# Fewer and larger transfers in a fused attention and state-space kernel

## The chip, the cores and the metric

The kernel runs on one core of one Trainium2 chip. The metric is the device time of one execution in microseconds (us). The engines of the core are PE (matrix multiplication), ACT (activation functions), DVE (elementwise work), POOL, and SP, whose instruction queue issues nearly all DMA transfers here. DMA transfers run beside the engines.

## The reference

Two branches of 2048 rows by 512 columns are mixed by a gate.

```python
g = sigmoid((x * gate_w).sum(-1, keepdims=True))
# branch A: attention, 32 heads of 16, no mask
q, k, v = split(x @ wqkv)
a = softmax(q @ k.T * 16 ** -0.5) @ v  @ wo
# branch B: state-space convolution of u = x over the sequence, per channel d
P = exp(dt * A * l)                      # powers l = 0..2047 of 128 states
K[d, l] = real(sum_n C[d,n] * P[d,n,l] * dt * B[d,n])
b = causal_conv(x, K) + x * Dskip        # written with an FFT
out = g * a + (1 - g) * b
```

Attention has 32 x 2048 x 2048 scores, and each needs an exponential. Branch B is computed in chunks of 64 rows: a short convolution inside the chunk ("taps"), a state per chunk that is carried on by a scan, and the state's part of the output by powers of the state matrix.

## The kernel before, in words

**Attention.** A block `b` (0 to 31) is 512 queries (`qc`) and four of a group of eight heads (`pi`, by parity `w`): 64 score tiles of 128 keys by 512 queries. The main loop (from line 1716) runs over 683 groups of three score tiles. `qk` (line 890) writes a group to PSUM with K = 32 matmuls: two heads of 16 rows share 32 rows, and `Qm` holds the queries of one of them, with zeros in the rows of the other. `ex` (line 905) is one ACT instruction, the exponential of the group's tiles. `pv` multiplies by V. Some tiles are taken from ACT: a "set" of four tiles is turned into bits of the exponential by DVE (`bits`, line 941, four instructions at line 945, and two at line 956). Which groups give a tile to DVE is settled by `decide` while the program is written, by the time that the planned DVE has left.

**Branch B.** `table` (line 1211) makes the powers of two blocks of 32 channels in `PT` and stores them in memory, `ptd`. `kstage` (line 1265) makes the taps of a block of 32 channels and stores them in `kpd`. `sstage` makes the chunk states, `scan` carries them on, in two halves of 8 blocks, on DVE. `ystage` (line 1384) is the output: 32 units of 16 channels. A unit needs its powers `Py` (from `ptd`), its taps `Tt` (from `kpd`, read as overlapping rows so that each partition is shifted by one), and `XY`, a turned copy of x for four blocks, from `xrd`. It makes 32 small matmuls with powers and 16 with taps into the PSUM bank `MB`, one DVE instruction (line 1420) into `Yst`, and stores to `ytd`, from which `yread` transposes into `Yl`. `turned` (line 1453) builds in memory, `xcd`, copies of x with zeros at their side, for the states.

**Order of the work.** Nothing is scheduled on the chip: the program of each engine is a fixed list, and an instruction waits on semaphores for what it reads. The lists are written by a planner (class `Sched`, line 282). Threads such as `ystage`, `yloads`, `qms`, `xyloads`, `turned` yield an engine and a cost; `fill` picks the piece that can start first by planned times, then by priority (line 1704: a smaller number goes first), and `AFTER` names a mark that must have been written already. The costs are the `c=` and `lat=` arguments, and a DMA is planned to be ready `DMARG` = 2.4 us later than that. So a change of a transfer's cost or number also changes where other work is put. After the writing, `place` finds addresses in SBUF by the life of each buffer. Where `want` finds too little matmul work, the planner puts in matmuls on zeros (`zero`, from `wm`).

The SP queue is one list in order. An SP instruction whose semaphore isn't there holds all that stand behind it. Loads of the Y stage have priority 4 and `XY` loads too; `ystage`'s own pieces, its stores among them, have 2; Q rows have 0.

Lines that the change touches: `yload` and `yloads` (1361 to 1382), the stores at 1426, `mk_qm` at 737, the store of Q at 1605, the taps' store at 1282, the zero stores at 1457 and the XR stores at 1467.

Of the kernel before, what the change touches and what calls it, by code (L numbers as in the profile page):

```python
# [13 lines left out]
P = 128  # L14
S = 2048
D = 512
# [24 lines left out]
YR = 4  # L41
# [373 lines left out]
def declare(nc, es):  # L415
# [89 lines left out]

    sb("Py", YR * 2 * 16 * T)
    sb("Tt", YR * 8 * 64)
# [6 lines left out]
    for n, free in (("ptd", NBLK * P * 2 * CB * T), ("kpd", NBLK * P * 8 * P), ("xrd", S * D), ("xcd", 2 * S * D), ("ytd", D * S), ("qd", D * S), ("od", D * S)):  # L514
        B[n] = Buf(n, "dr", free, BF16)
        B[n].t = nc.dram_tensor("gm_" + n, [free // P, P], BF16)
# [95 lines left out]
def record(nc, p, B, ins):  # L612
# [118 lines left out]
    def mk_qm(b, j):  # L731
# [4 lines left out]
        else:  # L736
            dma("SP", lambda e: e.dma_start(Qm(512 * w, [[1, 512]], 32 * j + 16 * w, 16),
                                            B["qd"].dram(((4 * qc + pi) * P + 32 * j + 16 * w) * 512, [[512, 16], [1, 512]])),
                [(B["qd"], (pi, qc))], [(Qm, (w, j), b)], c=.62, lat=2.8)
# [525 lines left out]
    def kstage(blk):  # L1265
# [16 lines left out]
        dma("SP", lambda e: e.dma_start(kpd.dram(blk * P * 8 * P, [[8 * P, P], [1, 8 * P]]), Kst(1024 * (blk % 2), [[1, 8 * P]])),  # L1282
# [76 lines left out]
    YN = 2 * 16 * T  # L1359

    def yload(u):
        blk, hf = divmod(u, 2)
        r = u % YR
        yield ("SP", .5)
        dma("SP", lambda e: e.dma_start(Py(r * YN, [[16 * T, 2], [1, 16 * T]]),
                                        ptd.dram(blk * P * PTN + hf * 16 * T, [[PTN, P], [CB * T, 2], [1, 16 * T]])),
            [(ptd, blk)], [(Py, r, u)], c=.62, lat=3.8)
        for par in range(2):
            for a in range(2):
                yield ("SP", .4)  # L1370
                dma("SP", lambda e, par=par, a=a: e.dma_start(  # L1371
                    Tt(r * 512 + 256 * a, [[64, 4], [1, 64]], 64 * par, 64),
                    kpd.dram(blk * P * 8 * P + (2 * hf + a) * 40 * 8 * P + par * 9 * P, [[1, 64], [18 * P, 4], [1, 64]])),
                    [(kpd, blk)], [(Tt, (r, par, a), u)], c=.64, lat=2.8)
        sch.mark(f"yl{u}")

    def yloads():
        yield ("AFTER", "S15")
        for u in range(2 * NBLK):
            if u >= YR:  # L1380
                yield ("AFTER", f"yu{u - YR}")
            yield from yload(u)

    def ystage():
        def unit(u):
# [3 lines left out]
            r, r2 = u % YR, u % 4  # L1389
            yield ("AFTER", f"scan{h}")  # L1390
            yield ("AFTER", "gt")
            yield ("AFTER", f"yl{u}")
# [7 lines left out]
            for q in range(4):  # L1400
                yield ("PE", .15)
                for ri in range(2):
                    for j in range(4):
# [3 lines left out]
                           lambda ri=ri, i=i: Py(r * YN + ri * 16 * T + i * T, [[1, T]]),  # L1407
                           [(sg, b_, (h, 'G')) for b_ in range(32)] + [(sg, "z"), (Py, r, u)], ky, False, False,
                           pos=(0, 32 * j), c=.075 if j == 0 else 0, a=16, cfg="C")
            for q in range(4):  # L1410
                yield ("PE", .09)
                for j in range(4):
# [3 lines left out]
                       lambda k=k, par=par: Tt(r * 512 + 64 * k, [[1, 64]], 64 * par, 64),  # L1416
                       [(B[f"XY{qr}"], par), (Tt, (r, par, k // 4), u)], ky, False, True, pos=(64 * par, 32 * j), c=.085 if j == 0 else 0, a=8,
# [6 lines left out]
            for par in range(2):  # L1424
                yield ("SP", .45)
                dma("SP", lambda e, par=par: e.dma_start(ytd.dram((256 * par + 8 * u) * S, [[T, 64], [2 * S, 4], [1, T]]), Yst(r2 * 256, [[64, 4], [1, 64]], 64 * par, 64)),
                    [(Yst, r2, u)], [(ytd, (u, par))], c=.6, lat=3.2)
# [390 lines left out]
```

## Time and profile before

| | |
|---|---|
| time, median of 3 runs | 838.77 us (838.6 to 840.81) |
| profiled execution | span 837.7 us; its own time isn't shown apart from the span |
| ACT busy | 819.1 us, 98% of the span |
| DVE busy | 783.3 us, 94% |
| PE busy | 698.3 us, 83% |
| PE granted clock, mean | 0.991 |
| DMA | 94.90 MB, 248465 packets, mean 113 GB/s |

The span runs from the first to the last instruction. "Busy" is the union of an engine's instructions; PE's share counts matmuls that overlap and that are there only to keep the engine at work. In the rows of groups stand the line, the engine, the operation, output and inputs by the program's names, shape and count; then busy time and mean duration of one in nanoseconds (two instructions can overlap, so busy divided by count is the pace); then the idle time of the engine just before, and what ended it. In the order of time, a row starts with its start and its length in us, and merges neighbours (x4); a bracket at its end is idle time before it. "SPq" is the issuing of a DMA by SP, not the transfer. Rows of stretches give, for each engine, busy us and number of instructions.

### The profile page before, as it was taken

The page shows a single profiled execution, that of the slowest core. Times are in us where ns is not written, and L with a number is a line of the kernel's source. Part 1 is how long each engine was busy: PE and PEld are TensorE (multiplying, and loading weights), DVE is VectorE, ACT ScalarE, POOL GpSimd, SP SyncE. Part 2 cuts the span into 40 slices and gives each one's busy share as a digit, 9 for nine tenths or more (in the row PEclk, how much of TensorE's full clock was granted, in tenths as well). Part 3 has the DMA queues.
Part 4 walks back from the last instruction along what each step waited for, and adds up shares of the span by engine and source line. Part 5 has one row for each costly group of instructions (what it writes and reads, how often), then busy time and mean ns, then how long its engine had stood idle before and what let it go on. Part 6 is the DMA issues. An engine that isn't in the chain of part 4 may idle for free.

```text
span 837.7 us, 21043 instructions
## 1 busy us (share of the span) xinstructions
PE 698.3 (83%) x8982; PEld 253.4 (30%) x8982; DVE 783.3 (94%) x1344; ACT 819.1 (98%) x695; POOL 11.0 (1%) x13
## 2 busy tenths in 40 slices
PE   7877777787679888887788887788897779999996
PEld 3232332122122332332232332244342224333332
DVE  5799999999889998999999999999899999999996
ACT  7999999999999999999999999999999999999996
POOL 4000000000000000000000000000000000000000
PEclk9999999999999999999999999999999999999999
DMA  9650044792361976873392846045564414544113
GB/s 207 142 83 10 23 77 92 202 228 57 128 177 46 223 123 179 119 205 67 139 144 40 143 67 143 1 108 136 140 148 109 115 54 110 135 99 132 34 45 101
DMA packets 248465, 94.90 MB, mean 113 GB/s; under 512 B 223156, under 2 KB 235316, under 8 KB 246324
## 3 DMA queue, kind: packets, MB, share of 16 engines
q1 hardware_dynamic: 246500, 92.51, 49.6%
q8 instruction: 70, 1.15, 0.5%
q10 hardware_dynamic: 1872, 1.05, 0.5%
q14 instruction: 23, 0.19, 0.1%
HBM read 33.08 MB, written 35.01 MB: 81 GB/s over the span
## 4 chain that ended last, share of the span: by engine, by line
ACT 83%; DVE 7%; PE 5%; DMA 3%; SPq 0%; issue 0%; ACTq 0%; DVEq 0%
ACT ET L909 83%; PE SC L628 2%; PE OA L628 2%; DVE tt L1006 2%; DMA gm_ptd<-PT 2%; DVE PT L1006 1%; DMA Wk<-in_A_wqkv_dram 1%; DVE DZ L945 1%; PE MB L628 1%; DMA XY<-gm_xrd 1%; DVE DZ L956 0%; DVE s L1336 0%; DVE OT L980 0%; DVE s L1338 0%; SPq L1371 0%
## 5 line engine op out<-in xcount | busy, mean ns | idle before, releaser
L909 ACT ACTIVATE ET<-SC 128x1536 bf16<-128x1536 f32 (+1 forms) x683 | 810.8, 1537 | 5.9 <-PE SC L628 3.6
L628 PE MATMUL SC<-Qm,KT 32*128 32x512 bf16 x2048 | 276.1, 387 | 122.4 <-ACT ET L909 107.7
L628 PE MATMUL OA<-wm 128*32 128x512 bf16 (+3 forms) x1374 | 204.1, 365 | 1.2 <-DVE wm L681 1.2
L945 DVE TENSOR_SCALAR DZ<-SC 128x512 uint16<-128x512 f32 x256 | 170.1, 684 | 10.3 <-PE SC L628 9.4
L628 PE MATMUL OA<-ET,VE 128*32 128x512 bf16 x1792 | 179.7, 394 | 0.0
L628 PEld LDWEIGHTS SC<-Qm,KT 32*128 32x128 bf16 x2048 | 70.9, 91 | 339.8 <-ACT ET L909 303.1
L628 PEld LDWEIGHTS OA<-ET,VE 128*32 128x32 bf16 x1792 | 45.7, 93 | 102.0 <-issue 97.6
L628 PEld LDWEIGHTS OA<-wm 128*32 128x32 bf16 (+2 forms) x1374 | 54.6, 95 | 25.9 <-issue 17.7
L956 DVE TENSOR_SCALAR DZ<-DZ 128x2048 uint16<-128x2048 uint16 x64 | 43.8, 684 | 3.0 <-PE OA L628 2.7
L1309 DVE TENSOR_SCALAR SG<-MB 128x512 bf16<-128x512 f32 x64 | 43.7, 684 | 3.0 <-DMA gm_ptd<-PT 1.7
L956 DVE TENSOR_SCALAR DU<-DZ 128x2048 uint16<-128x2048 uint16 x64 | 43.1, 684 | 0.1
L628 PE MATMUL MB<-X,Qt 128*128 128x64 bf16 x512 | 42.1, 244 | 1.2 <-DVE SG L1309 1.2
L1344 DVE TENSOR_TENSOR G<-s,s 128x512 f32<-128x512 f32 x60 | 41.3, 688 | 1.1
L1338 DVE TENSOR_TENSOR s<-G,MU 128x512 f32<-128x512 f32 x60 | 41.1, 684 | 0.0
L1341 DVE TENSOR_TENSOR s<-s,SG 128x512 f32<-128x512 f32 x60 | 41.0, 683 | 0.0
L1336 DVE TENSOR_TENSOR s<-G,MU 128x512 f32<-128x512 f32 x60 | 40.9, 682 | 0.0
L628 PEld LDWEIGHTS MB<-X,Qt 128*128 128x128 bf16 x512 | 28.8, 116 | 20.0 <-issue 20.0
L1006 DVE TENSOR_TENSOR ft<-FP,L 128x1024 f32<-128x1024 f32 (+1 forms) x32 | 34.4, 1086 | 0.2
L1006 DVE TENSOR_TENSOR PT<-tt,tt 128x1024 bf16<-128x1024 bf16 x48 | 32.9, 685 | 0.5
L628 PEld LDWEIGHTS MB<-Py,SG 128*32 128x32 bf16 x1024 | 27.8, 168 | 6.8 <-issue 4.1
L628 PE MATMUL MB<-Py,SG 128*32 128x64 bf16 x1024 | 28.6, 231 | 0.0
L1347 DVE CAST SG<-G 128x512 bf16<-128x512 f32 x60 | 25.3, 422 | 1.1
(167 smaller groups left out, 613.9 us busy)
## 6 DMA issues: line engine op xcount, KB each, us to landing
gm_ptd<-PT SPq DMA_DIRECT2D x16, 1024.0 KB, 5.9
Py<-gm_ptd SPq DMA_DIRECT2D x32, 512.0 KB, 4.3
gm_kpd<-Kst SPq DMA_DIRECT2D x16, 256.0 KB, 3.1
Tt<-gm_kpd SPq DMA_DIRECT2D x128, 32.0 KB, 3.2
gm_xrd<-in_A_x_dram SPq DMA_DIRECT2D x1, 2048.0 KB, 13.7
gm_xcd<-wm SPq DMA_DIRECT2D x4, 512.0 KB, 10.4
gm_xcd<-XR SPq DMA_DIRECT2D x32, 64.0 KB, 1.9
Wo<-in_A_wo_dram SPq DMA_DIRECT2D x4, 512.0 KB, 3.8
```

Of the source, the lines that this page charges most:

```text
L628: op("PE", lambda t: t.matmul(out(), lhsT(), rhs(), start=start, stop=stop, skip_group_check=True, **kw), R, W, c=c, lat=.15, a=a, cfg=cfg)
L909: op("ACT", lambda a: a.activation(ET(512 * e, [[1, 512 * n]]), sc(0, [[1, 512 * n]]), AF.Exp, scale=DH ** -0.5), [(sc, i, g) for i in ran ...
L945: op("DVE", lambda v: v.tensor_scalar(z.u16(512 * k, [[1, 512 * n]]), sc(512 * na, [[1, 512 * n]]), XS, XB, ALU.mult, ALU.add), [(sc, na + ...
L956: op("DVE", lambda v: v.tensor_scalar(t.u16(0, [[1, 2048]]), z.u16(0, [[1, 2048]]), float(STEP[k][0]), None, ALU.add), R, W, c=.07 + 2048 ...
L1006: op(eng, lambda v: v.tensor_tensor(o(), a(), b_(), f), R, W, c=c)
L1309: op("DVE", lambda v, kh=kh, part=part: v.tensor_scalar(sg(2 * SGH + SGH * part + CB * k8 + 16 * kh, [[2 * SGH, 32], [1, 16]]), MB(0, [[16 ...
L1336: op(e, lambda v: v.tensor_tensor(s2(0, W), G(0, W), MU(d0, [[0, 2], [1, 256]]), ALU.mult), key("G", "MU"), [(s2, 0)], c=F5)
L1338: op(e, lambda v: v.tensor_tensor(s3(0, W), G(256, [[-256, 2], [1, 256]]), MU(D + d0, [[D, 2], [1, 256]]), ALU.mult), key("G", "MU") + [(M ...
L1341: op(e, lambda v, so=so: v.tensor_tensor(s2(0, W), s2(0, W), sg(so, [[SGH, 2], [1, 256]]), ALU.add), [(s2, 0)] + ks, [(s2, 0)], c=F5)
L1344: op(e, lambda v: v.tensor_tensor(G(0, [[1, 512]]), s2(0, [[1, 512]]), s3(0, [[1, 512]]), ALU.add), [(s2, 0), (s3, 0)], [(G, 0)], c=F5)
L1347: op(e, lambda v, so=so: v.tensor_copy(sg(so, [[SGH, 2], [1, 256]]), G(0, W)), key("G"), ks if c < NCH - 2 else [(sg, k, (h, 'G')) for k i ...
```

## The change

1. **Taps and powers by blocks.** `yload` (per unit: one `Py` load of 512 KB, four `Tt` loads of 32 KB) is replaced by loads per block of two units: one `Py` load of 1 MB and two `Tt` loads, each 64 partitions by 16 channels. The ring holds two blocks where it held four units, in the same space; a block is loaded after the last unit of the block before last. For that, `kpd` is laid out with the 32 channels as outer rows.
2. **Outputs by two units.** `ytd` is stored once per block and half (two DMAs), after the second unit, where there were two DMAs per unit.
3. **Masked Q in one load.** `qd` is doubled: 16 rows of zeros stand behind the 16 rows of each head. One DMA loads all 128 partitions of `Qm`, zeros and data, where four DMAs loaded 16 rows each. A new thread, `gaps`, writes zeros once at the start (2 MB, over the gaps); a Q load reads both keys.
4. **Zeros of the turned x.** Four zero stores of 64-element rows, which left out the places of the data, become two stores of 512-element rows that cover everything (2 MB each); they are written after `blk2`, and the stores of `XR` now wait for them.

The diff, cut to its core:

```diff
-YR = 4
...
-    sb("Py", YR * 2 * 16 * T)
-    sb("Tt", YR * 8 * 64)
+    sb("Py", 2 * 2 * CB * T)
+    sb("Tt", 2 * 16 * 64)
...
-    def mk_qm(b, j):
+    def mk_qm(b):
...
-            dma("SP", lambda e: e.dma_start(Qm(512 * w, [[1, 512]], 32 * j + 16 * w, 16),
-                                            B["qd"].dram(((4 * qc + pi) * P + 32 * j + 16 * w) * 512, [[512, 16], [1, 512]])),
-                [(B["qd"], (pi, qc))], [(Qm, (w, j), b)], c=.62, lat=2.8)
+            dma("SP", lambda e: e.dma_start(Qm(512 * w, [[1, 512]]),
+                                            B["qd"].dram(((4 * qc + pi) * 256 + 16 * w) * 512, [[64 * 512, 4], [512, 32], [1, 512]])),
+                [(B["qd"], (pi, qc)), (B["qd"], "z")], [(Qm, (w, j), b) for j in range(4)], c=.62, lat=2.8)
...
-        dma("SP", lambda e: e.dma_start(kpd.dram(blk * P * 8 * P, [[8 * P, P], [1, 8 * P]]), Kst(1024 * (blk % 2), [[1, 8 * P]])),
+        dma("SP", lambda e: e.dma_start(kpd.dram(blk * P * 8 * P, [[8 * P, 4], [32 * P, 32], [1, 8 * P]]), Kst(1024 * (blk % 2), [[1, 8 * P]])),
...
     def yloads():
         yield ("AFTER", "S15")
-        for u in range(2 * NBLK):
-            if u >= YR:
-                yield ("AFTER", f"yu{u - YR}")
-            yield from yload(u)
+        for blk in range(NBLK):
+            r = blk % 2
+            if blk >= 2:
+                yield ("AFTER", f"yu{2 * blk - 3}")
+            yield ("SP", .5)
+            dma("SP", lambda e, blk=blk, r=r: e.dma_start(Py(r * PTN, [[1, PTN]]), ptd.dram(blk * P * PTN, [[PTN, P], [1, PTN]])),
+                [(ptd, blk)], [(Py, r, blk)], c=.66, lat=4.8)
+            for par in range(2):
+                yield ("SP", .4)
+                dma("SP", lambda e, blk=blk, r=r, par=par: e.dma_start(
+                    Tt(r * 1024, [[64, 16], [1, 64]], 64 * par, 64),
+                    kpd.dram(blk * P * 8 * P + par * 33 * P, [[1, 64], [66 * P, 16], [1, 64]])),
+                    [(kpd, blk)], [(Tt, (r, par), blk)], c=.66, lat=3.4)
+            sch.mark(f"yl{blk}")
...
-            for par in range(2):
-                yield ("SP", .45)
-                dma("SP", lambda e, par=par: e.dma_start(ytd.dram((256 * par + 8 * u) * S, [[T, 64], [2 * S, 4], [1, T]]), Yst(r2 * 256, [[64, 4], [1, 64]], 64 * par, 64)),
-                    [(Yst, r2, u)], [(ytd, (u, par))], c=.6, lat=3.2)
             if hf == 1:
+                for par in range(2):
+                    yield ("SP", .45)
+                    dma("SP", lambda e, par=par: e.dma_start(ytd.dram((256 * par + 16 * blk) * S, [[T, 64], [2 * S, 8], [1, T]]),
+                                                             Yst((r2 - 1) * 256, [[64, 8], [1, 64]], 64 * par, 64)),
+                        [(Yst, r2 - 1, u - 1), (Yst, r2, u)], [(ytd, (blk, par))], c=.66, lat=3.4)
...
+    def gaps():
+        yield ("SP", .7)
+        dma("SP", lambda e: e.dma_start(B["qd"].dram(16 * 512, [[32 * 512, P], [512, 16], [1, 512]]), wm(0, [[0, 16], [1, 512]])),
+            [(wm, 0)], [(B["qd"], "z")], c=1.4, lat=8.)
+
     def turned():
         XR, xcd = B["XR"], B["xcd"]
-        for z in range(4):
-            yield ("SP", .6)
-            dma("SP", lambda e, z=z: e.dma_start(xcd.dram(z // 2 * P * 8192 + z % 2 * 4096 + 64 * (1 - z % 2), [[8192, P], [P, 32], [1, 64]]), wm(0, [[0, 32], [1, 64]])),
-                [(wm, 0)], [(xcd, ("z", z))], c=.6, lat=6.)
+        yield ("AFTER", "blk2")
+        for z in range(2):
+            yield ("SP", 1.4)
+            dma("SP", lambda e, z=z: e.dma_start(xcd.dram(z * P * 8192, [[8192, P], [512, 16], [1, 512]]), wm(0, [[0, 16], [1, 512]])),
+                [(wm, 0)], [(xcd, ("z", z))], c=1.4, lat=10.)
         yield ("AFTER", XAT)
...
-                    [(XR, (c % 2, i), c) for i in range(2)], [(xcd, (c, cc))], c=.5, lat=3.)
+                    [(XR, (c % 2, i), c) for i in range(2)] + [(xcd, ("z", cc % 2))], [(xcd, (c, cc))], c=.5, lat=3.)
...
-                dma("SP", lambda e, i=i, c=c: e.dma_start(B["qd"].dram((4 * c + i) * P * 512, [[512, P], [1, 512]]), B["Qs"](512 * i, [[1, 512]])),
+                dma("SP", lambda e, i=i, c=c: e.dma_start(B["qd"].dram((4 * c + i) * 256 * 512, [[32 * 512, 8], [512, 16], [1, 512]]), B["Qs"](512 * i, [[1, 512]])),
...
-                for j in range(4):
-                    yield ("SP", .62, 0)
-                    mk_qm(b, j)
+                yield ("SP", .62, 0)
+                mk_qm(b)
...
-    for th, pr in ((norms(), 0), (qms(), 0), (projs(), 1), ...
+    for th, pr in ((norms(), 0), (gaps(), .9), (qms(), 0), (projs(), 1), ...
```

More of the change, by code (lines that the diff above doesn't have):

```diff
@@ L513, in declare @@
     B["MB"] = Buf("MB", "ps", 512, FP32)
-    for n, free in (("ptd", NBLK * P * 2 * CB * T), ("kpd", NBLK * P * 8 * P), ("xrd", S * D), ("xcd", 2 * S * D), ("ytd", D * S), ("qd", D * S), ("od", D * S)):
+    for n, free in (("ptd", NBLK * P * 2 * CB * T), ("kpd", NBLK * P * 8 * P), ("xrd", S * D), ("xcd", 2 * S * D), ("ytd", D * S), ("qd", 2 * D * S), ("od", D * S)):
         B[n] = Buf(n, "dr", free, BF16)
@@ L1441, in yread @@
             dma("SP", lambda e, par=par: e.dma_start_transpose(Yl(256 * par + 16 * blk, [[D, 16], [1, CB]]), ytd.dram((256 * par + 16 * blk) * S, [[S, CB], [1, S]])),
-                [(ytd, (2 * blk + u, par)) for u in range(4)], [(Yl, blk + par)], c=1.26, lat=1.6)
+                [(ytd, (blk + k, par)) for k in range(2)], [(Yl, blk + par)], c=1.26, lat=1.6)
             sch.mark(f"yr{blk + par}")
@@ L1477, in ublocks @@
             dma("SP", lambda e, blk=blk: e.dma_start_transpose(X2[blk % 4](0, [[1, 1024]]), B["xcd"].dram(blk * 16 * 8192, [[P, 1024], [1, P]])),
[L1478 removed]
+                [(B["xcd"], ("z", z)) for z in range(2)] + [(B["xcd"], (c, cc)) for c in range(8) for cc in range(4)], [(X2[blk % 4], 0, blk)], c=1.35, lat=3.3)
             sch.mark(f"ub{blk}")
```

33 lines of the change are left out of this document (8 added, 25 removed).

## The prediction

> **What bounds the kernel now.** I read the busy shares first.
>
> ```profile
> span 837.7 us, 21043 instructions
> ...
> PE 698.3 (83%) x8982; PEld 253.4 (30%) x8982; DVE 783.3 (94%) x1344; ACT 819.1 (98%) x695; POOL 11.0 (1%) x13
> ```
>
> ACT works 819.1 of 837.7 us. The profiled execution is shown by its span only; the median of the runs, 838.77, is 1.07 us more, and I carry that 1.07 along unchanged. A transfer can move the end in two ways only: it changes how much ACT has to do, or how long ACT waits. The groups by shape tell what ACT's work is made of.
>
> ```profile
> L909 ACT ACTIVATE ET<-SC 128x1536 bf16<-128x1536 f32 x426 | 582.8, 1756 | 1.9 <-PE SC L628 1.6
> L909 ACT ACTIVATE ET<-SC 128x1024 bf16<-128x1024 f32 x257 | 248.4, 1175 | 3.9 <-PE SC L628 2.0 <-PE OA L628 1.6
> L945 DVE TENSOR_SCALAR DZ<-SC 128x512 uint16<-128x512 f32 x256 | 170.1, 684 | 10.3 <-PE SC L628 9.4
> L956 DVE TENSOR_SCALAR DZ<-DZ 128x2048 uint16<-128x2048 uint16 x64 | 43.8, 684 | 3.0 <-PE OA L628 2.7
> L956 DVE TENSOR_SCALAR DU<-DZ 128x2048 uint16<-128x2048 uint16 x64 | 43.1, 684 | 0.1
> ```
>
> 683 exponentials on ACT hold three score tiles each (582.8/426 = 1.37 us) or two (248.4/257 = 0.97), so a tile that goes to DVE saves ACT 0.40 us. 256 tiles go there, in 64 sets of four. A set saves ACT 1.6 us and costs DVE (170.1 + 43.8 + 43.1)/64 = 4.0 us. How many sets there are is settled when the program is written out, from the time DVE has left. The busy time by stage says how much that is.
>
> ```profile
> 240.00:547.00 307.00, 256.73 (x3033) 89.95 (x3033) 295.56 (x507) 305.44 (x258) 1.05 (x2) 0.99 0.58 120
> 547.00:640.00 93.00, 81.38 (x1535) 36.18 (x1530) 89.53 (x162) 91.45 (x77) 0.00 (x0) 0.98 0.56 136
> 640.00:692.00 52.00, 40.31 (x477) 11.91 (x477) 50.08 (x90) 52.00 (x45) 0.00 (x0) 1.00 0.30 83
> 692.00:808.00 116.00, 109.86 (x1849) 44.84 (x1839) 110.96 (x192) 114.32 (x120) 0.00 (x0) 1.00 0.40 93
> ```
>
> Columns are PE, weight loads, DVE, ACT, POOL, then the granted clock, DMA share and rate. The second and fourth rows are the two halves of the Y stage (16 units each); DVE is idle 3.5 and 5.0 us in them, ACT 1.55 and 1.7. ACT's order of time puts that idle time into a few places.
>
> ```profile
> 594.34 1.02 ACT L909 ACTIVATE ET<-SC 128x1024 bf16<-128x1024 f32 x1 [0.56 <-PE SC L628]
> 596.07 1.02 ACT L909 ACTIVATE ET<-SC 128x1024 bf16<-128x1024 f32 x1 [0.71 <-PE SC L628]
> 597.38 153.56 ACT L909 ACTIVATE ET<-SC 128x1024 bf16<-128x1024 f32 x140 [0.28 <-PE SC L628]
> 751.14 19.77 ACT L909 ACTIVATE ET<-SC 128x1024 bf16<-128x1024 f32 x20 [0.20 <-PE OA L628]
> 771.42 18.44 ACT L909 ACTIVATE ET<-SC 128x1024 bf16<-128x1024 f32 x20 [0.50 <-PE OA L628]
> 790.50 1.94 ACT L909 ACTIVATE ET<-SC 128x1024 bf16<-128x1024 f32 x2 [0.64 <-PE OA L628]
> 792.66 36.03 ACT L909 ACTIVATE ET<-SC 128x1024 bf16<-128x1024 f32 x35 [0.23 <-PE OA L628]
> ```
>
> The bracket is ACT's wait before the row. First half: 0.56 + 0.71 + 0.28 = 1.55 us, all at 594. Second half: 1.57 us in four small waits. What made the wait at 594 is in the order of time of SP and PE.
>
> ```profile
> 565.87 0.62 SPq L1365 DMA_DIRECT2D Py<-gm_ptd  x1
> 566.53 2.60 SPq L1371 DMA_DIRECT2D Tt<-gm_kpd  x4
> 569.17 0.62 SPq L1449 DMA_DIRECT2D XY<-gm_xrd  x1
> 584.48 1.28 SPq L1426 DMA_DIRECT2D gm_ytd<-Yst  x2
> 588.43 0.62 SPq L1449 DMA_DIRECT2D XY<-gm_xrd  x1
> ```
>
> ```profile
> 593.20 0.44 PE L628 MATMUL MB<-Tt,XY 64*32 64x64 bf16 x14 [1.15 <-DMA XY<-gm_xrd]
> ```
>
> ```profile
> 594.00:598.00 4.00, 4.00 (x58) 1.28 (x54) 3.27 (x6) 2.67 (x3) 0.00 (x0) 0.58 0.74 204
> ```
>
> The two XY loads of a quarter are written one behind the other, but SP issued them 19 us apart, because it was issuing Y transfers without a pause. The second landed at 593.2, PE stood 1.15 us before the unit that needs it, the granted clock of the next 4 us was 0.58, and ACT lost the 1.55 us. It is the one place where a transfer that this change touches reaches ACT.
>
> **The change part by part.** Landing times come from the table of DMA issues (KB each, us to landing):
>
> ```profile
> gm_ptd<-PT SPq DMA_DIRECT2D x16, 1024.0 KB, 5.9
> Py<-gm_ptd SPq DMA_DIRECT2D x32, 512.0 KB, 4.3
> gm_xrd<-in_A_x_dram SPq DMA_DIRECT2D x1, 2048.0 KB, 13.7
> XY<-gm_xrd SPq DMA_DIRECT2D x8, 256.0 KB, 4.1
> gm_qd<-Qs SPq DMA_DIRECT2D x15, 128.0 KB, 2.2
> Qm<-gm_qd SPq DMA_DIRECT2D x120, 16.0 KB, 1.9
> ```
>
> *Y loads and stores.* A block (two units) cost SP 2 x (0.62 + 2.60) + 2 x 1.28 = 9.0 us; 16 units in the first half are 72 of its 93 us, and Q rows, XY and transposes fill most of the rest. Afterwards it is one Py, two Tt and two stores; at 0.62 us each, 3.1 us. The size of the pieces could raise that; a row that is four times as large in packets, XY, still takes 0.62. So about 8 x 5.9 = 47 us of SP time go from each half. On the path this is worth what the late XY cost: -1.55 us, because without the queue the second XY load is issued right behind the first, some 19 us earlier. The bounds are 0 (XY is late for another reason) and -1.55; I take -1.55.
>
> What is late next: the ring of loads becomes two blocks, so block n is loaded once both units of block n-2 are done, with two units to cover it (three before). Its price is three issues and a landing between XY's 4.1 and the 5.9 of the 1 MB rows: 6 to 8 us. Two units took 11.6 us in the first half (93/16 x 2) and 14.5 in the second, so it is hidden at today's pace. Without that cover the time of a Y step on PE is the bound:
>
> ```profile
> L628 PE MATMUL MB<-Py,SG 128*32 128x64 bf16 x1024 | 28.6, 231 | 0.0
> L628 PE MATMUL MB<-Tt,XY 64*32 64x64 bf16 x512 | 20.3, 234 | 1.2 <-DMA XY<-gm_xrd 1.2
> ```
>
> (28.6 + 20.3)/32 = 1.5 us a unit, 3.0 for two, so up to 5 us of waiting per block would come back, but as a wait of the Y thread, whose work is written later in its turn, not of PE: 0, with +1.55 as the other end, once, if a load lands after the point where it was planned. The pairing of stores delays the first unit's store by one unit; what reads it, the transposes into Yl, waits for four units anyway: 0.
>
> *Masked Q rows.* 120 issues become 30, each of 128 rows instead of 16; the nearest row is the store of the same 128 KB, 2.2 us to landing against 1.9: 0.3 us later, under a cover of one block of exponentials (21.3 x 1.37 = 29 us). Worth 0; without the cover, 30 x 2.2.
>
> *Zero rows and the turned x.* Start of the SP queue:
>
> ```profile
> 26.23 0.63 SPq L671 DMA_DIRECT2D gm_xrd<-in_A_x_dram  x1
> 26.90 20.07 SPq L1457 DMA_DIRECT2D gm_xcd<-wm  x4
> 47.01 2.96 SPq L1605 DMA_DIRECT2D gm_qd<-Qs  x1
> 52.25 1.73 SPq L737 DMA_DIRECT2D Qm<-gm_qd  x4
> 67.18 0.35 SPq L1605 DMA_DIRECT2D gm_qd<-Qs  x1
> 67.57 30.12 SPq L737 DMA_DIRECT2D Qm<-gm_qd  x8
> 104.53 2.05 SPq L1467 DMA_DIRECT2D gm_xcd<-XR  x4
> ```
>
> The four zero stores, 20.07 us of issuing, leave this place. One store of 2 MB in 1 KB rows takes it; its twin is the copy of x at 26.23: 0.63 to issue, 13.7 to land. Behind the copy it lands by about 27 + 2 x 13.7 = 54, and the first Q load, which now waits for it, comes at 54 instead of 52.25, for a block that opens after 67. The two new stores (2 MB each, bounded by 13.7 each: 27 us) follow, and the XR stores of 104.53 are the ones that now wait for them: done by 54 + 27 = 82. Cover 22 us, cost 0.
>
> *Powers.* The other order of rows in memory moves the same 256 KB stores and the same number of 128-byte packets: 0.
>
> Sum: 837.7 - 1.55 = 836.15 of span, with 1.07 around it 837.2.
>
> **The rivals.** *More sets on DVE.* With a pause of 1.35 us less at 594 and Y steps earlier, the writing-out may find room for more sets. For it: DVE is idle 3.5 + 1.9 + 5.0 us in 547 to 808, which is two sets of 4.0 us. Against it: that idle time is mostly in waits for scores, not for transfers. Two more: -1.55 - 3.2, 834.0.
>
> *The other side: Y steps bunch up on PE.* SP no longer paces the first half, so its units can come at well under 5.8 us and PE, 81.4 of 93 us busy, takes more small matmuls between two score tiles. In the second half, 109.9 of 116 us busy, this kind of crowding already cost ACT 1.57 us; and where PE dropped to clock 0.58, one event cost 1.55. It decides from three such events on: 838.8 - 1.55 + 3 x 1.55 = 841.9; four, 843.4. Against it: in the second half, the more crowded one, none of the four waits (0.20 to 0.64 us) came with a drop of the clock, which stands at 1.00 in its row. The Trainium skill (TensorE: Matmul & The Clock Gate, Part 1) says that the clock is halved after an idle window of some 3.4 us and comes back after a busy one as long; the 0.58 over 4 us agrees with the way back, while the pause that set it off is 1.15 us in the trace, shorter than the page asks for. By the page alone a crowd of small matmuls, being no pause, would keep the clock, and the sum would stay at 837.2.
>
> *Zero stores ahead of the Q load.* If the 4 MB of zeros enter the queue only at 67.57, just ahead of the loads for block 3, those land at 67.6 + 27.4 + 2.2 = 97.2, and block 3 opens at about 97 (the second four of the 67.57 row end at 97.7). Late by 0 to 1 us, plus one clock event: with the XY gain kept, 838.8 - 1.55 + 1 + 1.55 = 839.8; it decides once two blocks are hit: 839.8 + 2.5 (again up to 1 us and a clock event) = 842.3. The store at 47.01, whose issue took 2.96 against 0.35 at 67.18 in the same view, shows that a small store does stand behind zeros. The Trainium skill (DMA: Bandwidth & Descriptors, Queues, rings and completion order) says that an engine consumes descriptors in ring order, which is this rival's rule; no row here shows a Q load behind 4 MB.
>
> *Nothing comes of it.* The XY wait goes and another load is late once: 838.8.
>
> *Fewer sets.* The same mechanism as the first rival with the opposite sign; two fewer: 838.8 - 1.55 + 3.2 = 840.4; three, 842.0.
>
> **How the numbers follow.** Forecast 0.37, more sets 0.20, bunching (three events or more) 0.20, nothing 0.11, fewer sets 0.08, zeros first with two blocks hit 0.04. A difference of 0.3%, 2.5 us, is about what can be told from no change here (836.3 to 841.3). Faster: the 0.20 of more sets, and 0.07 of the forecast for one set more (835.6) = 0.27. Slower: bunching 0.20, half of fewer sets 0.04, zeros 0.04 = 0.28. The rest, 0.45, lies within. The predicted time is the forecast's 837.2, its own range 835.6 to 838.8. The range with the others goes from 833.8 to 843.5: it takes in two sets more and four clock events, and leaves out a tenth on each side.
>
> **What would show it.** SP free of back-to-back rows between 547 and 640; both XY loads of a quarter less than 2 us apart; no wait of PE for XY, and no clock below 0.9 at 590 to 600; 256 rows on L945 as now; four-fold fewer Q issues with landing near 2.2; zero stores landed before 100. The prediction is wrong if the count of L945 has moved by eight or more, if ACT's idle time between 547 and 808 is above 4 us, or if ACT waits near 69 or 97 us.

## The result and the profile after

The changed kernel takes 851.0 us (848.05 to 854.8 in six executions), the kernel before, run beside it, 839.72: a ratio of 1.0136, interval 1.0109 to 1.0163. The forecast was 837.2 with a range up to 843.5. It is slower by 11.3 us. The profiled execution is the fastest of the six, 848.05; all sums below are against its span, 846.2, and the 837.7 of the profile before. They explain those 8.5 us; the medians are 2.8 us further apart, and no trace covers that.

From the page of the changed kernel:

```profile
span 846.2 us, 20671 instructions
...
PE 697.6 (82%) x8966; PEld 250.1 (30%) x8966; DVE 780.3 (92%) x1338; ACT 820.6 (97%) x695; POOL 11.0 (1%) x13
```

The groups by shape (lines have moved up by one or two: L909 is L908 now, L945 is L944):

```profile
L908 ACT ACTIVATE ET<-SC 128x1536 bf16<-128x1536 f32 x430 | 589.4, 1738 | 11.1 <-PE SC L627 10.5
...
L908 ACT ACTIVATE ET<-SC 128x1024 bf16<-128x1024 f32 x253 | 245.1, 1218 | 1.0 <-PE SC L627 0.8
...
L944 DVE TENSOR_SCALAR DZ<-SC 128x512 uint16<-128x512 f32 x252 | 168.1, 684 | 9.7 <-PE SC L627 8.5
```

252 tiles on DVE instead of 256 is one set fewer: 1.6 us more for ACT. The busy time by stage, in the windows used for the prediction (PE, weight loads, DVE, ACT, POOL, clock, DMA share, rate):

```profile
547.00:640.00 93.00, 79.92 (x1567) 36.28 (x1559) 90.99 (x165) 93.00 (x77) 0.00 (x0) 1.00 0.63 148
...
692.00:808.00 116.00, 108.44 (x1860) 43.89 (x1857) 109.45 (x190) 116.00 (x121) 0.00 (x0) 1.00 0.42 96
...
594.00:598.00 4.00, 3.32 (x70) 1.54 (x67) 3.96 (x9) 4.00 (x4) 0.00 (x0) 1.00 0.24 39
```

Here the Y part did what was forecast and more: ACT is never idle in these stretches, and the clock at 594 stays at 1.00 (how much of that the change earned is told under "Why the prediction was wrong"). ACT's order of time shows where the loss is instead:

```profile
170.97 12.48 ACT L908 ACTIVATE ET<-SC 128x1536 bf16<-128x1536 f32 x9 [4.07 <-PE SC L627]
...
186.23 2.79 ACT L908 ACTIVATE ET<-SC 128x1536 bf16<-128x1536 f32 x2 [2.78 <-PE SC L627]
...
190.21 5.72 ACT L908 ACTIVATE ET<-SC 128x1536 bf16<-128x1536 f32 x4 [1.18 <-PE SC L627]
...
196.61 4.19 ACT L908 ACTIVATE ET<-SC 128x1536 bf16<-128x1536 f32 x3 [0.68 <-PE SC L627]
...
201.34 5.48 ACT L908 ACTIVATE ET<-SC 128x1536 bf16<-128x1536 f32 x4 [0.54 <-PE SC L627]
...
259.56 2.98 ACT L908 ACTIVATE ET<-SC 128x1024 bf16<-128x1024 f32 x3 [0.25 <-PE SC L627]
...
545.76 291.12 ACT L908 ACTIVATE ET<-SC 128x1536 bf16<-128x1536 f32 x266
```

Between 160 and 262 ACT waits 9.50 us. The kernel before waits once in that stretch:

```profile
190.91 5.48 ACT L909 ACTIVATE ET<-SC 128x1536 bf16<-128x1536 f32 x4 [0.68 <-PE SC L628]
```

So the difference of the spans, 8.5, is made of +8.8 (these waits), +1.6 (one set) and -3.1 (the waits of the two Y halves, 1.55 and 1.57, gone); the remaining 1.2 lies mostly at the start, where the first exponential comes at 12.61 instead of 11.57 behind the first loads (it isn't the change's: in the later runs it came anywhere from 11.11 to 12.86, and the 12.86 is that of e7 below, whose list of instructions is that of the kernel before).

What made PE late near 170 begins 60 us earlier, in SP's waits between 97 and 125 (us in total, times, longest):

```profile
SPq L262 <- PE MB L627: 12.1, 1, 12.1
```

and goes on in SP's order of time:

```profile
27.84 6.29 SPq L1447 DMA_DIRECT2D gm_qd<-wm  x1
...
45.03 0.59 SPq L736 DMA_DIRECT2D Qm<-gm_qd  x1
...
68.87 0.63 SPq L1455 DMA_DIRECT2D gm_xcd<-wm  x1
...
71.78 1.71 SPq L1455 DMA_DIRECT2D gm_xcd<-wm  x1
...
113.31 2.57 SPq L1461 DMA_TRANSPOSE XR<-gm_xrd  x2
...
158.47 0.93 SPq L1243 DMA_DIRECT2D gm_ptd<-PT  x2
...
174.07 5.70 SPq L1255 DMA_TRANSPOSE Qt<-gm_ptd  x1
...
179.81 0.59 SPq L1603 DMA_DIRECT2D gm_qd<-Qs  x1
...
567.31 3.21 SPq L1441 DMA_DIRECT2D XY<-gm_xrd  x2
...
590.38 4.38 SPq L1369 DMA_DIRECT2D Tt<-gm_kpd  x1
```

The first transpose of x into XR waits 12.1 us for PE and starts at 113.31. Everything behind it in SP's list is late by about as much: the first store of PT goes out at 158.47. In the kernel before the same two rows of SP are

```profile
99.89 3.11 SPq L1463 DMA_TRANSPOSE XR<-gm_xrd  x2
...
147.08 0.93 SPq L1244 DMA_DIRECT2D gm_ptd<-PT  x2
```

In the changed kernel DVE then waits for the store, and PE for DVE:

```profile
163.01 0.43 DVE L1226 COPY PT<-B 128x1024 bf16<-128x1024 bf16 x1 [3.09 <-DMA gm_ptd<-PT]
...
165.91 0.43 DVE L1226 COPY PT<-B 128x1024 bf16<-128x1024 bf16 x1 [2.48 <-DMA gm_ptd<-PT]
...
183.09 0.69 DVE L717 CAST Qs<-MB 128x512 bf16<-128x512 f32 x1 [2.56 <-DMA gm_qd<-Qs]
```

```profile
169.34 1.03 PE L627 MATMUL MB<-xT,Wq 128*128 128x512 bf16 x2 [4.35 <-DVE Qs L717]
```

Behind these matmuls stand the scores that ACT waits for, 4.07 us at 170.97. The second wait, 2.78 at 186.23, is the same shape: the store of Qs goes out only at 179.81, after a transpose that SP took 5.70 us to issue; DVE waits for that store, PE for DVE, ACT for PE. The chain that the profile follows back from 205 us is the same: a matmul into MB at 112.27, the transposes of XR, the stores of Qs and PT with DVE between them, the 5.70 us, PE, ACT.

Why should XR wait for PE? Once the order is written out, `place` gives every buffer its bytes; buffers whose lives do not overlap, counted in groups of the written order, may share them, and the first writer of a buffer then waits for the last readers of what lay there. The planner sets its times before that step and does not know of such waits. Before, XR (first used in group 81) lay on the bytes of L16, last used in group 60. The change makes no buffer larger or smaller: Py and Tt hold in two blocks what they held in four units. But it alters the order of the work, and with it the group in which 43 of the 141 buffers are first or last used. `place` searches for a packing of all of them, found another one, and 138 buffers have another address. XR now lies on Wk, whose last reader is a K projection of group 73. No line of the change speaks of XR's place.

### The profile page after: what moved, and what is told of

It is laid out like the page before. It is cut to its first block, busy times and chain, and to the rows that moved or that the text cites. A ratio compares the mean times of both kernels' runs of the same rounds, so it can differ in the third digit from the quotient of the medians.

```text
span 846.2 us, 20671 instructions
## 1 busy us (share of the span) xinstructions
PE 697.6 (82%) x8966; PEld 250.1 (30%) x8966; DVE 780.3 (92%) x1338; ACT 820.6 (97%) x695; POOL 11.0 (1%) x13
## 3 DMA queue, kind: packets, MB, share of 16 engines
q8 instruction: 70, 1.15, 0.6%
## 4 chain that ended last, share of the span: by engine, by line
ACT 77%; DVE 8%; DMA 6%; PE 4%; SPq 3%; issue 1%; ACTq 0%; DVEq 0%
ACT ET L908 77%; DMA gm_ptd<-PT 3%; DVE tt L1005 2%; PE SC L627 2%; PE OA L627 2%; DMA XR<-gm_xrd 1%; DMA gm_qd<-Qs 1%; DVE PT L1005 1%; SPq L1465 1%; DMA Wk<-in_A_wqkv_dram 1%; SPq L1461 1%; PE MB L627 1%; SPq L1255 1%; DVE DZ L944 1%; DVE ft L1005 0%
## 5 line engine op out<-in xcount | busy, mean ns | idle before, releaser
L908 ACT ACTIVATE ET<-SC 128x1536 bf16<-128x1536 f32 (+1 forms) x683 | 812.3, 1546 | 12.1 <-PE SC L627 11.3
L944 DVE TENSOR_SCALAR DZ<-SC 128x512 uint16<-128x512 f32 x252 | 168.1, 684 | 9.7 <-PE SC L627 8.5
L627 PEld LDWEIGHTS SC<-Qm,KT 32*128 32x128 bf16 x2048 | 68.9, 91 | 341.7 <-ACT ET L908 317.9
```

Source lines behind the costliest of these rows:

```text
L627: op("PE", lambda t: t.matmul(out(), lhsT(), rhs(), start=start, stop=stop, skip_group_check=True, **kw), R, W, c=c, lat=.15, a=a, cfg=cfg)
L908: op("ACT", lambda a: a.activation(ET(512 * e, [[1, 512 * n]]), sc(0, [[1, 512 * n]]), AF.Exp, scale=DH ** -0.5), [(sc, i, g) for i in ran ...
L944: op("DVE", lambda v: v.tensor_scalar(z.u16(512 * k, [[1, 512 * n]]), sc(512 * na, [[1, 512 * n]]), XS, XB, ALU.mult, ALU.add), [(sc, na + ...
```

## The experiments

Two theories stood at first: the late wait of XR for its bytes is the loss, or the merged and rearranged transfers are themselves slower. The runs are called e1 to e14 below.

**e1: the wait alone, put into the kernel before.**

```diff
         place(nc, bufs)
+        bufs["XR"].over.append(bufs["Wk"])   # XR also waits for Wk's last reader
```

> The kernel before, with one wait added: the first loads into XR also wait for the last reader of Wk, as they do in the changed kernel, where XR lies on the bytes of Wk. All transfers are those of before. Theory 1 (the shared bytes): XR begins at about 113 us instead of 99.9, the SP queue is late from there, the store of PT at 147 comes about 10 us later, DVE and PE stand behind it, and ACT waits 6 to 10 us between 160 and 205; 844 to 849 us. Theory 2 (the merged and enlarged transfers themselves are slow, 6 MB of zeros above all): none of them is here, so 838 to 840 us.

843.49 us, ratio 1.0053 (1.0038 to 1.0068), just under the 844 to 849 expected. SP's wait is that of the changed kernel, and ACT's largest wait comes at the same place; its waits are shorter:

```profile
SPq L263 <- PE MB L629: 12.4, 1, 12.4
```

```profile
169.27 24.45 ACT L910 ACTIVATE ET<-SC 128x1536 bf16<-128x1536 f32 x18 [3.48 <-PE SC L629]
...
194.59 4.25 ACT L910 ACTIVATE ET<-SC 128x1536 bf16<-128x1536 f32 x3 [0.87 <-PE SC L629]
...
199.49 1.45 ACT L910 ACTIVATE ET<-SC 128x1536 bf16<-128x1536 f32 x1 [0.66 <-PE SC L629]
```

A 12 us wait on a queue costs 3.6 us of the end. It is not the whole 11.3. The second large wait, 2.78 at 186.23, isn't here, nor is a transpose of Qt that takes 5.70 us to issue.

**e2: XR moved in the changed kernel.** `place` is told that XR lives from 20 groups earlier, so it can't lie on what has just died. All other addresses may move too.

```diff
-if o.first <= b.last + 1 and b.first <= o.last + 1)
+if o.first - lead(o) <= b.last + 1 and b.first - lead(b) <= o.last + 1)   # lead: 20 for XR, else 0
```

> The changed kernel, with XR placed as if it were in use 20 groups earlier, so that it can't lie on Wk; the lists of instructions are the same, the addresses of other buffers change too. Theory 1: XR begins at about 100, no wait of ACT above 1 us between 160 and 205, and the time is that of before less the wait for XY (1.55) plus one set fewer on DVE (1.6): 837 to 840 us. Theory 2: ACT's waits between 160 and 205 stay near 9 us, 846 to 852 us.

844.54, ratio 1.0062 (1.0047 to 1.0078): 6.5 us better than the changed kernel, but not back. The waits of 160 to 205 fall from 9.25 to 0.81, and a new one stands at 252:

```profile
252.15 2.79 ACT L910 ACTIVATE ET<-SC 128x1536 bf16<-128x1536 f32 x2 [6.59 <-PE SC L629]
```

```profile
237.83 0.43 DVE L1228 COPY PT<-B 128x1024 bf16<-128x1024 bf16 x1 [8.46 <-DMA gm_ptd<-PT]
```

The copy waits for a store of PT issued at 224.14. The packets of the stores show in the rate, 40 equal slices from 222 to 246:

```profile
GB/s 0 0 0 0 382 369 396 369 423 451 423 410 253 51 38 172 96 85 99 102 102 102 92 91 57 45 262 242 246 281 119 186 11 55 164 0 0 0 0 0
```

Both 1 MB stores of PT are over at about 230 at 400 GB/s. Behind them stand the stores of the powers, 2 x 256 KB, at about 100 GB/s. The semaphore records of the trace say how many of the 16 DMA engines report for each store, and when (the first of the powers' five, at 227.36, came before their first packet, at 229.65, so it tells of no data):

```
e2      PT      issued 224.14: 16 reports, 15 of them 229.97 to 230.18, the last 237.81
        powers  issued 226.41: 1 + 4 reports, 233.98 234.30 234.60 234.92
        (the second store of the powers: 1 + 4 reports, 237.75 to 237.77)
before  PT      issued 223.43: 16 reports, 15 of them 229.24 to 229.72, the last 231.22
        powers  issued 225.68: 16 reports, 229.95 to 231.84
```

The new order of rows gives the store an outer dimension of 4 (`[[8 * P, 4], [32 * P, 32], [1, 8 * P]]`), and 4 engines report for it. The Trainium skill (DMA: Bandwidth & Descriptors, "Why a DMA increments its semaphore by 16 and not by 1") has the rule: the number of engines is the largest up to 16 that divides the slowest dimension of both sides, and they are the lowest-numbered ones. These records agree with the number, 4; which engines they were they don't show. One report is late with each of these stores of PT (1.5 us in the kernel before). In e2 it came when the powers on four engines were through, though the last 8 KB packet of PT had ended at 231.44: it seems to have stood behind them, which no run isolates. It doesn't happen each time: in the profiled executions of the changed kernel and of e3, e7, e11 and e12, whose stores are as narrow, the report of the same store is 1.5 to 1.6 us late, as before.

**e3 and e4: parts of the change alone.** The Y part (loads and stores of the Y stage, powers in the new order of rows), and the larger zero stores:

> Parts 1 and 2 of the change alone (taps and powers by blocks, outputs by two units); XR doesn't lie on Wk here. Theory 1: the late XY load is gone (-1.55), and there is one set fewer on DVE (63, +1.6): 837 to 840 us, no wait of ACT at 160 to 205. Theory 2, if the larger loads are what costs: 844 us or more.

> Part 4 of the change alone (two large zero stores for the turned x, the XR stores wait for them); every buffer lies as before. Theory 1: nothing moves, 838 to 840 us. Theory 2, if the 4 MB of zeros are what costs: 842 us or more, with XR stores that wait at about 100.

The Y part gave 838.29, ratio 0.9994 (0.9965 to 1.0023), with executions from 834.28 to 843.73. XR lay on bytes last used in group 68, and its first transpose waited for DVE, until 104.93:

```profile
SPq L262 <- DVE MU L1041: 5.5, 1, 5.5
```

ACT has no wait between 93 and 243 there: 5.5 us on the queue were hidden. The zeros gave 838.77, 0.9989 (0.9972 to 1.0006). Neither alone holds the loss. The zeros of the turned x are settled: they cost nothing. (Those between the Q rows were not run alone.)

**e5, e6, e8: the powers stored in the old order, on 16 engines**, in the changed kernel, then with the wait added, then in the Y part alone:

```diff
-kpd.dram(blk * P * 8 * P, [[8 * P, 4], [32 * P, 32], [1, 8 * P]])
+kpd.dram(blk * P * 8 * P, [[8 * P, P], [1, 8 * P]])
-for par in range(2):                          # Tt: one load of 16 blocks
+for par in range(2): for g in range(4):       # Tt: four loads of 4 blocks
```

> Edit: the changed kernel, but the powers go to memory in the old order of rows (one outer dimension of 128 rows instead of 4 x 32), and each Tt is read by four loads instead of one. Three of 12 causes are told apart here and in the next run. The store of the powers (256 KB) moved some 100 GB/s in the changed kernel where it moved over 300 before, and its semaphore shows 4 landings in place of 16. The written-out program now has 64 sets on DVE again (63 in the changed kernel, worth 1.6 us of ACT), and XR lies on bytes that are free early. Theory N (the store on 4 of the 16 DMA engines makes the queue behind it late): the x transposes near 230 issue in about 6 us instead of 12, the loads of gq and gt land in about 2 instead of 4.5, no wait of ACT over 1 us between 160 and 262, time 836.5 to 838.5. Rival P (only where XR lies matters, and the rest is the chip's noise): x transposes stay at 10 to 12, time as in the changed kernel with XR moved less one set, 841 to 843. Rival M (the merged Q rows themselves are late): ACT waits over 2 us remain between 160 and 262, 842 or more.

> Edit: as the run before it, and the first load of XR also waits for the last reader of Wk (the wait that the changed kernel has from its shared bytes). With this the four cases are there: wait and narrow store (the changed kernel, 851.0), narrow store alone (844.5), wait alone (this), neither (the run before). Theory N with an effect of its own for the wait: as in the kernel before with that wait, +3 to +4.5 us over the run before it, 840 to 842.5, ACT waits in 160 to 205 of about 5 us, and no transposes of Qt that take 5.7 us to issue at 174. If the wait alone makes the whole loss (rival P): 846 or more, with some 9 us of ACT's waits in 160 to 205.

> Edit: the kernel before with the Y part alone (loads and stores of the Y stage merged), but the powers stored in the old order of rows and Tt read by four loads for each half. Theory N: x transposes at about 6 us, no late XY load, 64 sets; 835 to 837, that is 2 to 4.5 us under the kernel before, the Y gain of the prediction (1.55) and up to 2 more in the second half. Rival (the Y part gives nothing): 838.5 to 840.

848.21 (ratio 1.0133, 1.0093 to 1.0174), 849.28 and 848.94: no gain, against theory N, which each of them was to show. By its numbers e5 fits its rival M (late Q rows), but e8, whose Q rows are those of the kernel before, lost as much, so M isn't the reason. The rate did rise (the x transposes near 237 issue in 6.10 us instead of 12.18), but the edit moved the addresses once more. SP's wait between 100 and 125 in the first of them:

```profile
SPq L262 <- DVE nwi L1005: 13.6, 1, 13.6
```

XR now lay on u3, last read in group 74 by these rows of DVE. The premise of e5 (XR on early bytes) was false, and e6 added a wait for Wk to one that was there already, so it tells nothing new. ACT lost 3.54 + 0.87 + 0.91 us at 172 to 203, as in e1, and more on both sides of it.

**e9 and e10: the kernel of e5, XR kept free 20 groups ahead**, and the same for the Y part. In the first, the written order is that of e5; only addresses differ.

> Edit: as the run with the changed kernel and the wide store of the powers (848.2), but XR's bytes are kept free from 20 groups ahead, so that XR lies on none that died late. What that run showed: its store was wide (x transposes 6.1 us) and yet SP's first transpose of XR waited 13.6 us for the weight rows of the table, since XR lay on the bytes of u3, whose last reader is one of these operations. So this run is the fourth case: neither the wait nor the narrow store. Theory W (the wait of XR for bytes that another buffer holds late is the main loss, whichever buffer it is; the narrow store costs something only where a store of PT is caught behind it): SP's first XR transpose back at about 100, no ACT wait over 1 us between 140 and 262, 836 to 839. Rival S (shared bytes are not it; merging makes the start of the queue late in some other way): 843 or more, with ACT waiting in 140 to 262 again.

> Edit: the Y part alone with the wide store of the powers (848.9), XR's bytes kept free from 20 groups ahead. Theory W: 835.5 to 838.5, since the 13.8 us wait of the first XR transpose (for the weight rows) goes and with it the waits of ACT between 140 and 205 (2.07 + 0.62 + 3.13 + 0.86 + 0.66). Rival S: 843 or more. With the run before it, the difference is what the merged Q rows and zeros are worth; I expect under 1 us.

e9: 839.68, ratio 0.9985 (0.9965 to 1.0006): 8.5 us less than e5 by the medians, and 0.7 above the range of theory W. The first XR transpose is back:

```profile
99.81 2.57 SPq L1464 DMA_TRANSPOSE XR<-gm_xrd  x2
```

With the same list of instructions, then, other addresses alone are worth 8.5 us. Other buffers moved too, but XR's wait is the one that the traces follow to ACT and that e1 isolates; so its place is taken for the larger cause, though no run moves XR alone. e10 missed its expectation, 843.23 (1.0030, 1.0009 to 1.0052), though it is 5.7 us under e8, with e8's list; its trace has the Y stage short of Tt, where a block takes eight loads again:

```profile
615.64 0.27 PE L629 MATMUL MB<-Tt,XY 64*32 64x64 bf16 x2 [3.35 <-DMA Tt<-gm_kpd]
```

**e7: the narrow store alone in the kernel before** (the new order of rows, loads adapted, nothing merged), and **e11: XR at a third address in the changed kernel** (`lead` 10):

> Edit: the kernel before, with the powers stored in the new order of rows (4 x 32 outer dimensions) and the 128 Tt loads read from that order; no merge, the same instructions in the same order. Theory N: the rate of the store falls to about 100 GB/s, x transposes near 229 take 10 to 12 us to issue instead of 6.0, gq and gt land in 4 to 5 us instead of 2. What it costs in time depends on whether a store of PT gets caught behind it: 0 (as in the run with the Y part alone, 838.3) to +6.6 (as in the changed kernel with XR moved); I take +1, 840, range 838 to 846. Rival P: same as before in every row, 838.5 to 840.

> Edit: the changed kernel, its narrow store kept, with XR's bytes kept free from 10 groups ahead instead of 20: XR lies at another address again, on bytes whose last reader is at group 67 (14 groups ahead). Theory W: no 13 us wait of the first XR transpose, as with 20 groups. What is open is the second stall of that run (6.59 us of ACT at 252, a copy into PT that waited 8.46 us for the store of PT behind which narrow stores of the powers lay). If it belongs to the narrow store as such, it is there again: 843 to 845. If it hangs on which packets meet in that run's timing, it can be absent as in the Y part alone: 836 to 839. I take 60 to 40 for the first.

e7: 838.85, ratio 0.9998 (0.9989 to 1.0007). The transposes behind the store slow down as expected, and it costs nothing in that order of work and at those addresses, which are the ones of the kernel before:

```profile
229.49 10.84 SPq L1477 DMA_TRANSPOSE X<-gm_xcd  x4
```

e11: 846.0, ratio 1.0080 (1.0051 to 1.0109), but neither way that was expected. B16 of the third quarter now lay on Qs, and DVE stood for Qs's last store:

```profile
190.07 1.42 DVE L1007 TENSOR_TENSOR B<-ft,ft 128x512 bf16<-128x512 f32 x2 [6.73 <-DMA gm_qd<-Qs]
```

```profile
196.85 4.24 ACT L910 ACTIVATE ET<-SC 128x1536 bf16<-128x1536 f32 x3 [7.13 <-PE SC L629]
```

A wait of the same kind at another pair of buffers: it says more on addresses than on the store.

**e12 to e14: the narrow store put back into e9, and taken out of e2 and e3.** In e12 the instructions, their order and all SBUF addresses are e9's; in e13 they are e2's, and in e14 e3's, except that the store is split into four of 32 rows each.

```diff
-[[8 * P, 4], [32 * P, 32], [1, 8 * P]]                             # e2: one store, 4 engines
+for g in range(4): ... + 8 * P * g, [[32 * P, 32], [1, 8 * P]]     # e13: four stores, 16 engines each
```

> Edit: the fourth case (no late wait of XR, wide store; 839.68) with one thing put back: the powers are stored in the new order of rows again (4 x 32), the Tt loads read from that order. The instructions of all engines, their order and every address in SBUF stay. Theory N2 (the store on four DMA engines is a cause of its own: a store of PT whose last part is caught behind it comes late, and the copy into PT with it): x transposes at 10 to 12 us instead of 6, a wait of DVE for the store of PT of 5 to 9 us near 230, ACT waiting some 6 us near 245, 844 to 846. Rival C (in the changed kernel with XR moved that stall came from something else): 839 to 841, no such wait.

> Edit: the changed kernel with XR moved (844.54), the store of the powers split into four of 32 rows each, in the new order of rows, so that none has an outer dimension of 4. Written-out order and addresses stay; SP issues three stores more per block. Theory N2: the 8.46 us wait of the copy into PT at 237.8 goes to 3 or less, ACT's 6.59 us at 252 go, 837 to 839.5. Rival C: the 6.6 us stay, 843.5 to 846.

> Edit: the Y part alone (838.29, 834 to 844 in ten executions, 834.28 in its profile), with the store of the powers split into four of 32 rows each. It has neither of the two causes, and one set of DVE fewer than the kernel before. Theory N2: the profile's 834 becomes the rule, 834 to 836.5. If the spread of that run had another reason: 838 to 839, as before.

e12: 845.11, ratio 1.0072 (1.0048 to 1.0095), 5.4 us over e9. e13: 839.99, 0.9996 (0.9975 to 1.0018), 4.6 us under e2 and 0.5 above its expectation, and the wait for the store of PT is 1.81 us at most. What is left of ACT's waits in e13 is mostly in the Y stage, where a block's loads came late:

```profile
611.99 1.45 ACT L910 ACTIVATE ET<-SC 128x1536 bf16<-128x1536 f32 x1 [1.89 <-PE SC L629]
613.87 2.97 ACT L910 ACTIVATE ET<-SC 128x1536 bf16<-128x1536 f32 x2 [0.42 <-PE SC L629]
617.09 212.96 ACT L910 ACTIVATE ET<-SC 128x1536 bf16<-128x1536 f32 x203 [0.26 <-PE SC L629]
```

```profile
603.32 3.78 SPq L1372 DMA_DIRECT2D Tt<-gm_kpd  x1
```

```profile
611.13 0.28 PE L629 MATMUL MB<-Tt,XY 64*32 64x64 bf16 x2 [2.12 <-DMA Tt<-gm_kpd]
```

Both runs say that the narrow store costs about 5 us in the merged kernel, at two sets of addresses. It does not cost it in every execution: e12's executions go from 840.38 to 850.41 (e9's from 837.4 to 841.95), and its profiled one is the fastest, with the x transposes at 11.25 us but no late report. So the late report is seen in e2's trace alone, the price in e12's and e13's times; that the slow executions of e12 have that report is not shown. Why the order of the kernel before (e7) is spared is open; so is what the merged Q rows, which are in e2, e9, e12 and e13 and not in e7, have to do with it. They are narrow as well: in the changed kernel each Q load, with an outer dimension of 4, has 1 + 4 reports (29 of 30 in the records), the last 4.2 us after the issue by the median, where the loads of 16 rows had 16 reports in 1.9; each store of Qs, with one of 8, has 1 + 8, in 3.3 us where it took 2.0. e9 and e13 keep these and take no longer than the kernel before.

e14, the Y part alone with the store in four, has no narrow store, and XR's wait is the 5.5 us that e3 hides: 836.54 (834.91 to 838.98 in twelve), ratio 0.9966 (0.9953 to 0.9980). It is 0.3% under the kernel before. From 128.68 to the end of the exponentials ACT waits three times:

```profile
243.88 78.26 ACT L908 ACTIVATE ET<-SC 128x1536 bf16<-128x1536 f32 x68 [0.16 <-PE SC L627]
...
322.85 95.44 ACT L908 ACTIVATE ET<-SC 128x1536 bf16<-128x1536 f32 x83 [0.71 <-PE SC L627]
...
418.76 406.34 ACT L908 ACTIVATE ET<-SC 128x1024 bf16<-128x1024 f32 x360 [0.47 <-PE SC L627]
```

## Why the prediction was wrong

- *The XY wait, -1.55*: the mechanism was right, the size was that of one execution. Both XY loads of a quarter go out in one row (567.31, x2), no wait, clock 1.00. But e1, e4 and e7 keep the Y transfers of the kernel before, with the XY loads 18 to 19 us apart, and ACT lost 0.94, 0 and 0 us there in place of 1.55. The granted clock goes with it: it stood at 0.5 for 3.41 us after a pause of PE of 1.15 us in the kernel before, and after one of 0.73 in e1, and at 1.00 after the 0.52 of e4; e7 had no pause. The four waits of the second half, 1.57 us, not counted as a gain, stand in all these runs (1.55 to 1.57) and went with the change. In e4 PE waited for XY and ACT, from 420 to 749, did not wait:

```profile
592.59 0.42 PE L628 MATMUL MB<-Tt,XY 64*32 64x64 bf16 x14 [0.52 <-DMA XY<-gm_xrd]
```

```profile
420.00 329.05 ACT L909 ACTIVATE ET<-SC 128x1024 bf16<-128x1024 f32 x283 [0.47 <-PE SC L628]
```

- *SP time per block, 9.0 to 3.1*: the sign was right, the size not. Merged transfers did not issue in 0.62 us: a Tt load took 1.50 on the mean between 547 and 640, up to 4.38 (the row at 590.38), and a store to `ytd` 1.14. The eight blocks loaded and stored there cost SP 49.6 us, 6.2 each; the same transfers had taken 75.0 of that stretch, so some 25 us went and not 47, and SP was not free of back-to-back rows. The price of a load of a block, "6 to 8 us", was too low with it: in e13 the loads of one block were issued from 598.60 on, the last at 603.32, and PE had them at 611.13, 12.5 us later, where two units cover 11.6. That cost 1.89 + 0.42 + 0.26 us of ACT, and the eight-load form 3.35 us of PE in one place: the other end of the two-block ring, "+1.55 once", is real, though the changed kernel did not meet it.
- *Powers, "the same 256 KB stores and the same number of 128-byte packets: 0"*: the first step that failed. Bytes and packets were the same, the number of DMA engines was not: 4 instead of 16, 100 GB/s where the same store of the kernel before reaches 374 in the slices near 200. Its price in the merged kernel is 4.6 to 5.4 us by the two pairs. The diff shows it: the outer dimension of 4 is written there.
- *Zero rows and the turned x, "the XR stores of 104.53 are the ones that now wait for them ... cost 0"*: the zeros of the turned x were indeed hidden (e4), and the first Q load, behind the zeros between the Q rows, came at 45.03, earlier than the 54 forecast. But the row that mattered is the one ahead, the transposes into XR at 99.89. The prediction took it that what an instruction waits for is named in the code around it; XR's wait came from its address. This is the second step that failed, and the larger: 8.5 us between e5 and e9, 6.5 between the changed kernel and e2, 5.7 between e8 and e10, 3.6 in e1.
- *Sets*: one fewer, +1.6, a smaller case of the last rival (two fewer, 840.4).
- *Masked Q rows, 0*: not settled. The term leaned on a store of 128 KB with 16 reports, "2.2 us to landing"; the merged load has 4 and takes 4.2. With the store wide and XR moved, the whole change stands at 0.9996 (e13). e13 is 3.5 us over e14, which has neither the merged Q rows nor the larger zeros. In the profiles, 5.4 us apart, 2.6 of that is the Y wait at 612; the addresses differ too, and what the Q rows cost or bring stays open.
- *The rivals*: none had this mechanism. "A wait that takes the place of the one removed" was looked for behind the edited transfers only. The signs listed for a wrong prediction would not have found it either: ACT's idle time after 547 is 0, nothing happens near 69 or 97, and the count of L944 moved by four. No sign looked at 160 to 262.
- The two causes together: 851.0 with both, 844.5 with the narrow store alone (e2), 848.2 with a late wait of XR alone (e5, another buffer and one set more), 839.7 with neither (e9). They overlap: each makes DVE wait for a store of PT, and with it PE and ACT. In the profiled execution of the changed kernel the narrow store's part is not a late report but, it seems, the transpose of Qt that took 5.70 us to issue behind two narrow stores; the first one took 1.25 in e5, behind wide ones.

## What to carry to other kernels

When addresses are found by the lives of buffers, a change of the order of work alone moves them. Look at what every buffer's bytes held before, not only at the code that was edited: a first write onto bytes that died late is a wait that this plan did not show, and 12 to 14 us of it on a queue cost 3.6 to 8.5 us at the end here, while 5.5 us cost nothing that shows. When a transfer is rearranged, compare the outermost dimension of both sides as well as the bytes; splitting one store of 4 x 32 rows into four of 32 brought it back to all engines. When a part of a change tests well alone, look at the addresses it ran with before giving the loss to the other part. And before a single wait is counted as a gain, see whether a second execution has it.

## What the runs showed of the hardware

- A 256 KB store with an outer dimension of 4 is reported by 4 DMA engines and moves about 100 GB/s; with 128 rows it is reported by 16, and split into four of 32 rows, each part is too. A load with an outer dimension of 4 (Q rows, 128 KB) is reported by 4, a store with one of 8 by 8. Four x transposes issued behind two such stores took 10.7 to 12.7 us to issue, against 5.2 to 6.2 behind wide ones.
- A store that is done on 15 engines at 230.18 was reported by the last one at 237.81, 7.6 us later, when the narrow stores behind it were through (e2); that these made it late is not isolated. In five other profiles with narrow stores that report was 1.5 to 1.6 us late.
- The 2 MB store of zeros between the Q rows took SP 6.29 us to issue at 27.84, right behind the copy of x; the two stores of the same size at 68.87 and 71.78 took 0.63 and 1.71. Whether its pieces or what lay ahead of it made the difference is not shown.
